# Three pairs' q, k and v in one transfer each, ahead of a unit's stores, with the v casts moved into the Mish stretch

## The chip, the cores and the metric

The kernel runs on one core of a Trainium2 chip. The metric is device time of the whole kernel in microseconds (us); lower is better. The engines are named as the profile names them: PE is TensorE (PEld its weight loads), DVE is VectorE, ACT is ScalarE, POOL is GpSimd, SP is SyncE, which issues nearly all DMA transfers.

## The reference

Attention over 8 batches, 12 heads, 448 positions and a head size of 64, with an extra `exp(-m)` in the softmax's denominator, followed by a two-layer network with Mish between the layers (768 to 2048 to 768, on 3584 tokens). Inputs and output are float32.

```python
scale = 1.0 / np.sqrt(q.shape[-1])
scores = scale * np.matmul(q, k.transpose(0, 1, 3, 2))
m = np.max(scores, axis=-1, keepdims=True)
e = np.exp(scores - m)
attn = e / (np.sum(e, axis=-1, keepdims=True) + np.exp(-m) + 1e-09)
attn_out = np.matmul(attn, v)
x = attn_out.transpose(0, 2, 1, 3).reshape(B * S, H * D)
h = x @ w_in
sp = np.where(h > 20.0, h, np.log1p(np.exp(np.minimum(h, 20.0))))
out = (h * np.tanh(sp)) @ w_out
```

## The kernel before, in words

Work goes by pairs of heads: 48 pairs (`N_PAIRS`), six to a batch. Three pairs (`UNIT_PAIRS`) make a unit, so a batch has two units and the kernel 16 (`N_UNITS`), numbered here from `u` = 0. After a head of two units done pair by pair, each pass of the loop over `u` does three things at once: the scores, maxima, exponentials and sums of unit `u`; the product of its predecessor's attention with v (line 423); and pieces of the network for earlier batches, which fill TensorE between the scores (`fill`, line 543 for the second layer). The second half of a unit is the Mish stretch: eight steps `f`, each with six products of line 442 and a Mish on ScalarE (line 481), between which the next unit is made ready. The order on every engine is the order of the program text (`tc.manual_schedule()`); from the seventh unit on (`u` = 6, `JOINED_FROM`) the first half of a unit follows a list written by hand, `JOINED`.

A pair's way into a unit:

- `load_pair` (line 149) issues three transfers on SP, for q, k and v, 224 KB each (112 partitions, 2 heads, runs of 1 KB), into tiles of a pool with four buffers. In the units with `u` over 4 (`first_mm2`), all the three pairs of the next unit are loaded, one each at the three entries `("load", 0)`, `("load", 1)` and `("load", 2)` of `JOINED` (in the sixth unit, at steps 0, 3 and 6). The stores of finished output rows (line 507) come from the same queue, at the entries `copy`.
- `cast_pair` (line 190) turns q, k and v into bf16 on POOL, in that order (lines 201 or 203, 207 and 188). The first pair is cast at the second load entry, the second pair at the third, the third pair at step `f` = 1 of the Mish stretch.
- q and k are then transposed, either by eight matmuls on TensorE (line 224; four for q, then four for k), at `f` = 3 for the second pair and at `f` = 5 for the third, or by one DMA on SP (`turn_by_dma`, line 237), which a unit's first pair takes from the eighth unit on (turned in the unit before it). In the last unit the second pair goes by DMA too. `rest_of` (lines 245 and 246) copies two small blocks of each pair on POOL.

A unit's own weights leave by `normalise` (line 369): seven operations on DVE (line 386) for the first pair at `f` = 0, seven for the second at `f` = 3, and seven on POOL (line 384) for the third at `f` = 4. Each is followed by a DMA transposition into `eT` on SP (line 390). So SP's queue holds, for each unit in turn: loads, stores, the turned pair, three `eT` transpositions, and then the next unit's loads.

Of the kernel before, what the change touches and what calls it, by code (L numbers as in the profile page):

```python
# [9 lines left out]
FP32 = mybir.dt.float32  # L10
# [5 lines left out]
UNIT_PAIRS = 3  # L16
# [3 lines left out]
def kernel(  # L20
# [11 lines left out]
    B, H, S, D = q.shape  # L32
# [3 lines left out]
    NT = 4  # L36
    SP_ = S // NT
# [10 lines left out]
    N_PAIRS = B * HP  # L48
# [4 lines left out]
    def pool(name, bufs, space=None):  # L53
        if space is None:
            return ctx.enter_context(tc.tile_pool(name=name, bufs=bufs))
        return ctx.enter_context(tc.tile_pool(name=name, bufs=bufs, space=space))

    PS = bass.MemoryType.PSUM
    singles = pool("singles", 1)
    ld_pool = pool("ld", 4)  # L60
    bf_pool = pool("bf", 9)
    st_pool = pool("st", 5)
    eT_pool = pool("eT", 3)
# [36 lines left out]
    w_in_sb = singles.tile([128, DM_T, d_ff], BF16)  # L100
    w_out_sb = singles.tile([128, FF_T, d_model], BF16)

    N_CAST = 2 * UNIT_PAIRS
    qk_bf = singles.tile([SP_, N_CAST, 2, NT, 2, D], BF16)
    qk_all = singles.tile([128, UNIT_PAIRS, 2, S], BF16)
# [26 lines left out]
    loaded, casted, qkT, att, xT, gT, o_sbs, stats = {}, {}, {}, {}, {}, {}, {}, {}  # L132
# [13 lines left out]
        return mo_free.popleft()  # L146


    def load_pair(p, which="qkv"):
        if p >= N_PAIRS:  # L150
            return
        b, h0 = p // HP, (p % HP) * 2
        tiles = loaded.setdefault(p, [])
        for nm, src in (("q", q), ("k", k), ("v", v)):
            if nm not in which:
                continue
            t = ld_pool.tile([SP_, 2, NT * D], FP32, tag=f"{nm}_f", name=f"{nm}_f")
            nc.sync.dma_start(
                out=t, in_=src[b, h0 : h0 + 2].rearrange("h (p t) d -> p h (t d)", t=NT)
            )  # L160
            tiles.append(t)


    def w_pieces():
# [21 lines left out]

    def cast_v(p):
        nc.gpsimd.tensor_copy(out=casted[p][2], in_=loaded.pop(p)[2])  # L188

    def cast_pair(p, with_v=True):  # L190
        if p >= N_PAIRS:
            return
        q_f, k_f = loaded[p][:2]
        q_bf, k_bf = (qk_bf[:, p % N_CAST, i] for i in range(2))
        v_bf = bf_pool.tile([SP_, 2, NT * D], BF16, tag="v_bf", name="v_bf")
        by_t = "p h (t d) -> p t h d"
        cast_q, cast_k = nc.gpsimd.tensor_copy, nc.gpsimd.tensor_copy
        if p == 0:
            cast_q, cast_k = nc.vector.tensor_copy, nc.scalar.copy
        if p not in SCALED_IN_CAST:  # L200
            cast_q(out=q_bf, in_=q_f.rearrange(by_t, t=NT))  # L201
        else:
            nc.gpsimd.tensor_scalar(  # L203
                out=q_bf, in0=q_f.rearrange(by_t, t=NT),
                scalar1=SCALE, scalar2=1.0, op0=ALU.mult, op1=ALU.mult,
            )
        cast_k(out=k_bf, in_=k_f.rearrange(by_t, t=NT))  # L207
        casted[p] = (q_bf, k_bf, v_bf)
        if with_v:
            cast_v(p)  # L210
# [23 lines left out]
    def turn_by_dma(p):  # L234
# [331 lines left out]
    first_mm2 = 2 * UNITS_PER_B  # L566
# [85 lines left out]
    LEAD = UNIT_PAIRS + 1  # L652
    LOAD_AT = (0, 3, 6)
# [33 lines left out]
    for p in range(UNIT_PAIRS):  # L687
        cast_v(p)
# [32 lines left out]
    for u in range(UNITS_PER_B, N_UNITS + 2 * UNITS_PER_B):  # L721
# [10 lines left out]
        nxt = p0 + UNIT_PAIRS  # L732
# [5 lines left out]
        for what, arg in JOINED if joined else ():  # L738
            at, idx = p0 + arg, p0 * STEPS + arg
            heads = {"A": (0,), "B": (1,)}.get(what[-1], (0, 1))  # L740
            if what == "s":
                held[arg] = score_products(idx)
            elif what[0] == "m":
                score_maxima(*held[arg], heads)
            elif what[0] == "e":
                exps(idx, heads)
            elif what == "fill":
                for _ in range(arg):
                    filler.popleft()[0]()
            elif what == "copy":  # L750
                for evac in copies[arg]:
                    evac()
            elif what == "av":
                held["av", arg] = av_pair(at - UNIT_PAIRS, bank=joined_banks[AV_BANK[arg]])
            elif what == "avc":
                held["av", arg]()
            elif what == "load":
                load_pair(at + LEAD - 1)
                if arg:
                    cast_pair(at + LEAD - 2)  # L760
            elif nxt + arg in TURN_BY_DMA:
                turn_by_dma(nxt + arg)
        if joined:
# [2 lines left out]
        for n in () if joined else range(steps):  # L766
            pi, s = divmod(n, STEPS)
            p, idx = p0 + pi, p0 * STEPS + n
            late_tp = u == UNITS_PER_B and n == STEPS
            if late_tp:  # L770
                transpose_pair(p0 + 2)
            exps(idx)
            if grouped:
                order = GROUPED_LATE_AV if u == LATE_AV else GROUPED
                flush_late()
                for what, arg in order[n]:
                    if what == "fill":
                        for _ in range(min(arg, len(filler))):
                            fn, w = filler.popleft()
                            fn()  # L780
                            done += w
                    elif what in ("av0", "av1"):
                        late.append(av_pair(p0 - UNIT_PAIRS + arg, bank=sc_banks[int(what[2])][0]))
                    else:
                        flush_late()
                        for i in arg:
                            scores(p0 * STEPS + i)
                if n in LOAD_AT:
                    at = p0 + LOAD_AT.index(n)
                    if u > first_mm2:  # L790
                        load_pair(at + LEAD - 1)
                        if n:
                            cast_pair(at + LEAD - 2)
                    elif n < LOAD_AT[-1]:
                        load_pair(at + LEAD)
                        cast_pair(at + LEAD - 1)
                if u - UNITS_PER_B < len(W_AT):
                    load_w(W_AT[u - UNITS_PER_B].get(n, 0))
                if n in TURN_AFTER and nxt + TURN_AFTER.index(n) in TURN_BY_DMA:
                    turn_by_dma(nxt + TURN_AFTER.index(n))  # L800
                continue
            if late_tp:
                evac_qk(p0 + 2, act=True)
            if u == UNITS_PER_B + 1:
                for i, part in enumerate(TURN_AT[1].get(n, [])):
                    turn_on_pe(*part)
                    if n == 0:
                        mm1_ahead(0, FIRST_AHEAD[i])
            flush_late()
            acc += weight[n]  # L810
            want = int(total * acc / sum(weight) + 1e-6)
            while done < want:
                fn, w = filler.popleft()
                fn()
                done += w
            scores_ahead(end)
            if n in LOAD_AT:
                load_pair(p0 + LOAD_AT.index(n) + LEAD)
                cast_pair(p0 + LOAD_AT.index(n) + LEAD - 1)
            if u - UNITS_PER_B < len(AV_AT):  # L820
                early = AV_AT[u - UNITS_PER_B]
                if n in early:
                    late.append(av_pair(early[n], act=early[n] in AV_BY_ACT))
                if u == UNITS_PER_B:
                    for part in TURN_AT[0].get(n, []):
# [9 lines left out]
        b, w = (u - UNITS_PER_B) // UNITS_PER_B, u % UNITS_PER_B  # L835
# [5 lines left out]
        for f in range(FF_U):  # L841
# [4 lines left out]
            if moe:  # L846
# [4 lines left out]
                elif to_group:  # L851
                    at = (FIRST_MISH_BANK if first else MISH_BANK)[f]
# [73 lines left out]
```

## Time and profile before

| What | Value |
|---|---|
| median of 3 runs | 462.56 us (461.56 to 463.87) |
| the profiled execution, its own time | 464.11 us |
| its span on the core | 462.3 us |
| PE busy | 427.4 us (92%) |
| DVE, ACT, POOL busy | 340.9, 342.1, 187.3 us |
| granted TensorE clock over the run | 0.987 |
| read from and written to HBM | 45.61 MB, 11.01 MB |

The span is what the trace covers; the profiled execution's own time is 1.8 us longer. The profile's views used below are the page's first part (busy time by engine), the windows (busy time of each engine in a stretch), the timeline of one engine (start and length in us, then what it is, and in brackets how long the engine was idle before and what released it), and the instructions of one line. Times in windows and timelines count from the span's start.

### The profile page before, as it was taken

Reading aid. Unit: us, or ns where it says so; the run is one execution under the profiler, and the core shown is the slowest. Engines: PE = TensorE matmul, PEld = TensorE weight load, DVE = VectorE, ACT = ScalarE, POOL = GpSimd, SP = SyncE. Lnnn points to the kernel's source line nnn. Section 1 sums busy time; section 2 is a strip of 40 time slices with the busy share of each in tenths; the row PEclk is TensorE's granted clock in tenths of the full one; section 3 lists DMA queues with packets and bytes.
Section 4 is the critical chain, followed back from the end, with each engine's and each line's share of the span. In section 5 each row is a group of like instructions: output and inputs, shape, how many; then the busy total and the mean of one; then the engine's idle time right before and its main releaser. Section 6 shows DMA issues by size and latency. Waiting matters only on the chain.

```text
span 462.3 us, 8732 instructions
## 1 busy us (share of the span) xinstructions
PE 427.4 (92%) x2968; PEld 234.3 (51%) x2968; DVE 340.9 (74%) x756; ACT 342.1 (74%) x908; POOL 187.3 (41%) x352
## 2 busy tenths in 40 slices
PE   4596798869999999899999999999999999999996
PEld 2243445434545655455555555455555455555565
DVE  4899978948887888868788888788888888421121
ACT  5998978967797979778888788798988888311300
POOL 4666655652616253353627171625454360000000
PEclk9997999999999999999999999999999999999999
DMA  8999999999999999999999999999999995950213
GB/s 229 207 200 221 255 151 215 221 199 216 195 246 238 207 210 204 264 194 278 199 244 231 219 234 209 271 206 238 227 270 205 255 203 137 171 137 0 69 35 102
DMA packets 211661, 92.66 MB, mean 200 GB/s; under 512 B 168352, under 2 KB 208160, under 8 KB 211616
## 3 DMA queue, kind: packets, MB, share of 16 engines
q1 hardware_dynamic: 204032, 85.76, 87.9%
q0 software_dynamic: 7488, 6.29, 9.4%
q8 instruction: 23, 0.38, 0.4%
q14 instruction: 22, 0.18, 0.1%
q10 hardware_dynamic: 96, 0.05, 0.0%
HBM read 45.61 MB, written 11.01 MB: 122 GB/s over the span
## 4 chain that ended last, share of the span: by engine, by line
PE 65%; DMA 16%; DVE 5%; ACT 5%; issue 3%; SPq 3%; POOL 2%; POOLq 0%; DVEq 0%; ACTq 0%
PE mo L543 25%; PE mo L442 15%; DMA q_f<-in_q_dram 7%; PE b L442 6%; PE b L543 5%; PE b L304 4%; ACT en L347 4%; DMA k_f<-in_k_dram 4%; DMA eT<-en 4%; DVE negm L335 3%; PE b L423 2%; PE mo L423 2%; PE b L224 2%; DMA qk_all<-qk_bf 1%; SPq L390 1%
## 5 line engine op out<-in xcount | busy, mean ns | idle before, releaser
L347 ACT ACTIVATE en<-b,negm 128x448 bf16<-128x448 f32 x216 | 133.9, 636 | 25.7 <-DVE negm L335 25.7
L335 DVE TENSOR_REDUCE negm<-b 128x1 f32<-128x448 f32 x216 | 120.9, 616 | 20.0 <-PE b L307 20.0
L543 PE MATMUL mo<-w_out_sb,gT 128*128 128x384 bf16 (+3 forms) x736 | 108.7, 300 | 1.4 <-DVE o_sb L522 0.7
L543 PEld LDWEIGHTS <-gT 128*128 128x128 bf16 x896 | 82.6, 98 | 51.8 <-issue 10.8
L442 PEld LDWEIGHTS <-w_in_sb 128*128 128x128 bf16 x768 | 72.3, 98 | 66.5 <-issue 5.5
L442 PE MATMUL mo<-xT,w_in_sb 128*128 128x448 bf16 x480 | 101.1, 353 | 0.8 <-DVE xT L432 0.3
L481 ACT ACTIVATE gT<-mo 128x448 bf16<-128x448 f32 x73 | 40.3, 552 | 52.1 <-PE mo L442 52.0
L384 POOL TENSOR_SCALAR en<-en,rden 128x448 bf16<-128x448 bf16 x109 | 67.3, 634 | 19.5 <-DVE rden L378 11.8
L386 DVE TENSOR_SCALAR en<-en,rden 128x448 bf16<-128x448 bf16 x227 | 71.8, 386 | 0.7
L442 PE MATMUL b<-xT,w_in_sb 128*128 128x448 bf16 x282 | 58.7, 352 | 0.0
L347 ACT ACTIVATE en<-sc,negm 128x448 bf16<-128x448 f32 x84 | 52.5, 642 | 3.9 <-DVE negm L335 2.6
L522 DVE COPY o_sb<-mo 128x384 f32<-128x384 f32 (+3 forms) x54 | 25.8, 494 | 40.1 <-PE mo L543 39.4
L335 DVE TENSOR_REDUCE negm<-sc 128x2 f32<-128x896 f32 (+1 forms) x48 | 45.4, 969 | 6.4 <-PE sc L307 4.0
L203 POOL TENSOR_SCALAR qk_bf<-q_f 112x512 bf16<-112x512 f32 x18 | 11.1, 615 | 88.1 <-DMA q_f<-in_q_dram 88.1
L347 ACT ACTIVATION_READ_ACCUMULATOR en<-b,negm 128x1 f32 x216 | 45.0, 208 | 0.0
L201 POOL CAST qk_bf<-q_f 112x512 bf16<-112x512 f32 x29 | 19.7, 679 | 44.6 <-DMA q_f<-in_q_dram 44.2
L188 POOL CAST v_bf<-v_f 112x512 bf16<-112x512 f32 x48 | 30.1, 626 | 15.0 <-DMA v_f<-in_v_dram 14.7
L207 POOL CAST qk_bf<-k_f 112x512 bf16<-112x512 f32 x47 | 29.3, 623 | 7.6 <-DMA k_f<-in_k_dram 6.4
L423 PEld LDWEIGHTS <-v_bf 112*64 112x64 bf16 x384 | 20.1, 110 | 23.4 <-issue 9.0
L224 PEld LDWEIGHTS <-qk_bf 112*128 112x128 bf16 x304 | 19.6, 104 | 21.7 <-POOL qk_bf L207 4.6
L304 PE MATMUL b<-qk_all 64*128 64x448 bf16 x108 | 29.3, 358 | 0.3 <-DMA qk_all<-qk_bf 0.3
L307 PE MATMUL b<-qk_all 64*128 64x448 bf16 x108 | 29.3, 358 | 0.0
(71 smaller groups left out, 524.7 us busy)
## 6 DMA issues: line engine op xcount, KB each, us to landing
q_f<-in_q_dram SPq DMA_DIRECT2D x48, 224.0 KB, 5.4
k_f<-in_k_dram SPq DMA_DIRECT2D x48, 224.0 KB, 5.6
v_f<-in_v_dram SPq DMA_DIRECT2D x48, 224.0 KB, 5.6
w_in_sb<-in_moe_w_in_dram POOLq DMA_DIRECT2D x12, 256.0 KB, 6.3
w_out_sb<-in_moe_w_out_dram POOLq DMA_DIRECT2D x8, 384.0 KB, 6.9
out_dram<-o_sb SPq DMA_DIRECT2D x7, 336.0 KB, 5.2
out_dram<-o_sb SPq DMA_DIRECT2D x8, 288.0 KB, 4.9
out_dram<-o_sb SPq DMA_DIRECT2D x8, 240.0 KB, 5.2
```

The costliest lines, as they stand in the source:

```text
L188: nc.gpsimd.tensor_copy(out=casted[p][2], in_=loaded.pop(p)[2])
L207: cast_k(out=k_bf, in_=k_f.rearrange(by_t, t=NT))
L304: nc.tensor.matmul(sc[0][:, 0:S], lhsT=qT[0:64, qa : qa + 128], rhs=kA, start=True, stop=True)
L307: nc.tensor.matmul(sc[1][:, 0:S], lhsT=qT[64:128, qb : qb + 128], rhs=kB, start=True, stop=True)
L335: nc.vector.tensor_reduce(out=negm, in_=scored, axis=AX.X, op=ALU.max, negate=True)
L347: nc.scalar.activation(out=st["en"][:, :, c, 0:SP_], in_=sc[bk][:, 0:S].rearrange("q (j c) -> q j c", j=NT), func=AF.Exp, bias=st["negm"][ ...
L384: nc.gpsimd.tensor_scalar(scalar2=1.0, op0=ALU.mult, op1=ALU.mult, **args)
L386: nc.vector.tensor_scalar(scalar2=None, op0=ALU.mult, **args)
L423: nc.tensor.matmul(av[h * 64 : (h + 1) * 64, 0:S], lhsT=v_bf[:, h, j * D : (j + 1) * D], rhs=e_h, start=(j == 0), stop=(j == NT - 1),)
L442: nc.tensor.matmul(h_ps[:, 0:S], lhsT=w_in_sb[:, dm, ff * 128 : (ff + 1) * 128], rhs=xT[b][:, dm, :], start=(dm == 0), stop=(dm == DM_T - 1),)
L481: nc.scalar.activation(out=gT[b][:, ff, :], in_=h_ps[:, 0:S], func=AF.Mish)
L543: nc.tensor.matmul(st["o"][:, st["at"] : st["at"] + nq * NQ], lhsT=src[:, ff, c0 : c0 + 128], rhs=w_out_sb[:, ff, q0 * NQ : (q0 + nq) * NQ ...
```

## The change

The pool of load tiles is replaced by one tile each for q, k and v with four slots. In the units from the sixth on (`u` over 4) the first load entry issues one transfer for q, one for k and one for v, each for all three pairs of the next unit (672 KB); the two other load entries issue none. The second entry casts q and k of the first pair, the third entry q and k of the second and third pairs. The three v casts come at `f` = 1 of the Mish stretch, where the third pair's casts stood. Units before the sixth load and cast as they did, into the slots. On PE, DVE and ACT the instructions and their order are the same in both kernels; SP issues 60 fewer loads, and POOL's casts come in the order q, k, q, k, q, k, v, v, v.

```diff
-    ld_pool = pool("ld", 4)
...
+    N_LD = UNIT_PAIRS + 1
+    ld = {
+        nm: singles.tile([SP_, N_LD, 2, NT * D], FP32, tag=f"{nm}_f", name=f"{nm}_f")
+        for nm in "qkv"
+    }
...
-    def load_pair(p, which="qkv"):
+    def load_pair(p, which="qkv", pairs=1):
...
-        tiles = loaded.setdefault(p, [])
+        at = 0 if pairs > 1 else p % N_LD
...
             nc.sync.dma_start(
-                out=t, in_=src[b, h0 : h0 + 2].rearrange("h (p t) d -> p h (t d)", t=NT)
-            )
-            tiles.append(t)
+                out=ld[nm][:, at : at + pairs].rearrange("p s h x -> p (s h) x"),
+                in_=src[b, h0 : h0 + 2 * pairs].rearrange("h (p t) d -> p h (t d)", t=NT),
+            )
+            for i in range(pairs):
+                loaded.setdefault(p + i, []).append(ld[nm][:, at + i])
...
+    def load_and_cast(nxt, step):
+
+        if nxt >= N_PAIRS:
+            return
+        if step == 0:
+            load_pair(nxt, pairs=UNIT_PAIRS)
+        elif step == 1:
+            cast_pair(nxt, with_v=False)
+        else:
+            for p in range(nxt + 1, nxt + UNIT_PAIRS):
+                cast_pair(p, with_v=False)
...
             elif what == "load":
-                load_pair(at + LEAD - 1)
-                if arg:
-                    cast_pair(at + LEAD - 2)
+                load_and_cast(nxt, arg)
...
                     if u > first_mm2:
-                        load_pair(at + LEAD - 1)
-                        if n:
-                            cast_pair(at + LEAD - 2)
+                        load_and_cast(nxt, LOAD_AT.index(n))
...
-                if f == 1 and u >= first_mm2:
+                if f == 1 and u == first_mm2:
                     cast_pair(nxt + UNIT_PAIRS - 1)
+                elif f == 1 and u > first_mm2 and nxt < N_PAIRS:
+                    for p in range(nxt, nxt + UNIT_PAIRS):
+                        cast_v(p)
```

More of the change, by code (lines that the diff above doesn't have):

```diff
@@ L156, in load_pair @@
                 continue
-            t = ld_pool.tile([SP_, 2, NT * D], FP32, tag=f"{nm}_f", name=f"{nm}_f")
             nc.sync.dma_start(
-                out=t, in_=src[b, h0 : h0 + 2].rearrange("h (p t) d -> p h (t d)", t=NT)
-            )
-            tiles.append(t)
+                out=ld[nm][:, at : at + pairs].rearrange("p s h x -> p (s h) x"),
+                in_=src[b, h0 : h0 + 2 * pairs].rearrange("h (p t) d -> p h (t d)", t=NT),
+            )
+            for i in range(pairs):
+                loaded.setdefault(p + i, []).append(ld[nm][:, at + i])
     def w_pieces():
```

## The prediction

> **What bounds the kernel now.** I read the page first, then the stretches of nine like units, then one unit in order of time, engine by engine.
>
> ```profile
> span 462.3 us, 8732 instructions
> PE 427.4 (92%) x2968; PEld 234.3 (51%) x2968; DVE 340.9 (74%) x756; ACT 342.1 (74%) x908; POOL 187.3 (41%) x352
> ```
>
> TensorE is busy 92% of the span, so a change of loads can only give back the gaps between TensorE's work, or add to them. The stretches run from one unit's first `mo` product of line 543 to the next unit's, for the seventh to the fifteenth unit; the columns are length, then the busy time of each engine.
>
> ```profile
> 149.74:174.15 24.41, 24.41 (x174) 13.55 (x175) 21.11 (x49) 20.91 (x57) 9.93 (x21) 1.00 1.01 205
> 174.15:200.58 26.43, 24.74 (x174) 13.47 (x175) 20.53 (x48) 21.01 (x57) 12.22 (x24) 1.00 1.08 239
> 275.10:300.26 25.16, 24.57 (x175) 13.55 (x175) 21.01 (x48) 21.01 (x57) 11.65 (x24) 1.00 1.16 236
> sum 224.48, PE 220.80 PEld 121.20 DVE 188.30 ACT 188.37 POOL 101.34; mean PE 24.53 PEld 13.47 DVE 20.92 ACT 20.93 POOL 11.26
> ```
>
> A unit without a wait takes 24.41 us (first row). Nine take 224.48, so 224.48 - 9 x 24.41 = 4.8 us, 0.53 a unit, is all that the nine lose. Where it is lost is seen in the unit of the third row, in the DMA queue of SP:
>
> ```profile
> 270.38 13.56 SPq L390 DMA_TRANSPOSE eT<-en  x3
> 284.00 0.57 SPq L158 DMA_DIRECT2D q_f<-in_q_dram  x1
> ...
> 286.61 0.46 SPq L158 DMA_DIRECT2D v_f<-in_v_dram  x1
> 287.17 2.27 SPq L507 DMA_DIRECT2D out_dram<-o_sb  x4
> 289.74 0.66 SPq L158 DMA_DIRECT2D q_f<-in_q_dram  x1
> 290.67 0.34 SPq L158 DMA_DIRECT2D k_f<-in_k_dram  x1
> 291.60 0.31 SPq L158 DMA_DIRECT2D v_f<-in_v_dram  x1
> 292.27 1.26 SPq L237 DMA_TRANSPOSE qk_all<-qk_bf  x1
> 295.20 13.73 SPq L390 DMA_TRANSPOSE eT<-en  x3
> 308.98 0.57 SPq L158 DMA_DIRECT2D q_f<-in_q_dram  x1
> ```
>
> The first load leaves the moment the third `eT` transposition has been issued. I call this T0 (284.00) and count from it. Two pairs' loads leave by +3.1, then four stores, and the third pair's only at +5.7 to +7.9. The three `eT` transpositions hold SP for 13.73 us; the next T0 follows at once. So T0 is set by the first `eT`, and that by the first normalisation. POOL and TensorE in the same unit:
>
> ```profile
> 287.86 0.62 POOL L203 TENSOR_SCALAR qk_bf<-q_f 112x512 bf16<-112x512 f32 x1 [9.21 <-DMA q_f<-in_q_dram]
> 288.79 0.61 POOL L207 CAST qk_bf<-k_f 112x512 bf16<-112x512 f32 x1 [0.31 <-DMA k_f<-in_k_dram]
> 289.84 0.61 POOL L188 CAST v_bf<-v_f 112x512 bf16<-112x512 f32 x1 [0.44 <-DMA v_f<-in_v_dram]
> 290.71 0.61 POOL L201 CAST qk_bf<-q_f 112x512 bf16<-112x512 f32 x1 [0.26 <-DMA q_f<-in_q_dram]
> 291.64 0.61 POOL L207 CAST qk_bf<-k_f 112x512 bf16<-112x512 f32 x1 [0.31 <-DMA k_f<-in_k_dram]
> 292.32 0.61 POOL L188 CAST v_bf<-v_f 112x512 bf16<-112x512 f32 x1
> 295.19 0.61 POOL L201 CAST qk_bf<-q_f 112x512 bf16<-112x512 f32 x1 [2.26 <-DMA q_f<-in_q_dram]
> 296.14 0.75 POOL L207 CAST qk_bf<-k_f 112x512 bf16<-112x512 f32 x1 [0.34 <-DMA k_f<-in_k_dram]
> 296.84 0.65 POOL L188 CAST v_bf<-v_f 112x512 bf16<-112x512 f32 x1
> ```
>
> ```profile
> 293.33 0.56 PE L224 MATMUL b<-ident,qk_bf 112*128 112x112 bf16 x8
> ...
> 296.00 0.36 PE L224 MATMUL b<-ident,qk_bf 112*128 112x112 bf16 x4
> 296.95 0.37 PE L224 MATMUL b<-ident,qk_bf 112*128 112x112 bf16 x4 [0.59 <-POOL qk_bf L207]
> ```
>
> The second pair's k was cast by 292.25 (+8.3), its transposes came at +9.3, without a wait. The third pair's k was cast at 296.89, and TensorE stood 0.59 us for it. This is the wait that the change is aimed at.
>
> **What goes.** The third pair's q and k no longer queue behind stores, and the v casts no longer lie between the q and k casts. At best this wait goes in all nine units: 4.8 us, 1.0%. Fewer instructions on SP (three loads for nine) give nothing by themselves: T0 hangs on the `eT` chain. If the issue of a transfer three times as large took three times as long, 1.4 us for 0.46, three would be out at +4.2, still before the stores are needed. The stores leave earlier or at the same place in the queue, and nothing waits for them.
>
> **What moves later: the second pair.** All casts are in POOL's order q0, k0, q1, k1, q2, k2, and k0 now waits for the whole k transfer: the sixth piece of 224 KB on the queue. The nearest rows for when six pieces have landed are in the seventh unit, whose loads began at 157.88:
>
> ```profile
> 157.88 0.57 SPq L158 DMA_DIRECT2D q_f<-in_q_dram  x1
> ...
> 161.45 0.62 POOL L203 TENSOR_SCALAR qk_bf<-q_f 112x512 bf16<-112x512 f32 x1 [9.18 <-DMA q_f<-in_q_dram]
> ...
> 164.08 0.61 POOL L188 CAST v_bf<-v_f 112x512 bf16<-112x512 f32 x1 [1.36 <-DMA v_f<-in_v_dram]
> ...
> 166.36 0.61 POOL L188 CAST v_bf<-v_f 112x512 bf16<-112x512 f32 x1 [0.20 <-DMA v_f<-in_v_dram]
> ```
>
> POOL was waiting for v of the first pair (third piece) until +6.2 and for v of the second (sixth piece) until +8.5; in the unit above the fifth piece was there at +7.6 and the sixth by +8.3. I take +8.2 for k, between 7.6 and 8.5, and 10.6 for v, at the same pace (2.4 us for three pieces). Then k0, q1, k1 at 0.62: k1 is ready at 8.2 + 3 x 0.62 + 0.1 for two hand-overs (296.89 to 296.95 is one) = 10.1, where TensorE wants it at 9.53 (293.33 plus 0.2 for the first four). That is a wait of 0.57 at the second pair, with the 0.59 at the third gone: k2 is ready at 11.4, before the third pair comes. One wait takes the place of another, worth +0.04 a unit against today's mean of 0.53.
>
> The bigger transfer could be cheaper. The Trainium skill's "DMA: Bandwidth & Descriptors" (section "Anatomy of one DMA — SWDGE (gpsimd) path") fits a DMA's time as 2.0 us plus bytes by 436 GB/s: by it q would land at 3.6 and k at 5.2. The rows do not agree: by that fit three pieces behind each other would also be there at 3.6, and they took 5.8 and 6.2.
>
> **What gets dense: POOL beside the first normalisation.** Today POOL rests from 292.93 to 295.19, and the first normalisation of DVE lies just there; the second lies beside casts:
>
> ```profile
> 293.32 1.81 DVE L386 TENSOR_SCALAR en<-en,rden 128x448 bf16<-128x448 bf16 x7
> ...
> 295.35 2.78 DVE L386 TENSOR_SCALAR en<-en,rden 128x448 bf16<-128x448 bf16 x7
> ```
>
> ```profile
> L386 DVE TENSOR_SCALAR en<-en,rden x3: 323/677/678, 245.8 to 246.6; 128x448 bf16<-128x448 bf16 x3
> ```
>
> Seven take 1.81 us alone, 2.78 beside about three casts. In the unit at 245.8 those beside a cast took 0.677, those clear of one 0.323: 0.35 us for each. After the change POOL casts without a break from 8.25: five to 11.4, and the three v casts after them to 13.3. The first normalisation starts at 9.3 (293.32), in the middle of it. If all seven meet a cast it takes 7 x 0.35 = 2.45 us longer; none, 0. Call this x. The first `eT`, today 0.07 us behind it (295.13 to 295.20), is late by x, and so is the next T0 with all its loads. The second normalisation meets casts today too, so I put nothing there; the turn of the first pair (line 237) waits for k0, 8.9 for 8.27, and ends at 10.2, before the first `eT`.
>
> The Trainium skill's "SBUF — State Buffer" (section "Who interferes with whom") says that such a DVE operation and a POOL one lock each other out for a whole instruction. By turns of 0.61 and 0.26 (1.81 for seven) each of the seven would then take 0.87, and x would be 4.3. The rows agree that DVE is held up, but a held one takes 0.677, waiting and all, and the casts grow only to 0.65 to 0.75, so I keep 2.45 as the top.
>
> **The sum.** Let TensorE come to the second pair's k at A after T0, and wait s = 10.1 - A. The next T0 lies at A - 0.21 (start of the normalisation) + 1.81 + x + 0.07 + 13.78 (295.20 to 308.98) = A + 15.45 + x; TensorE comes to its next second pair at A + s + 24.41. So the next A = 8.96 + s - x. In balance A = 9.53 - x/2 and s = 0.57 + x/2. Half of any delay of T0 is paid in each unit, as TensorE's wait also moves the next normalisation. Against today's 0.53 a unit the nine units lose 9 x (0.04 + x/2).
>
> x = 0 gives +0.4 us, x = 2.45 gives +11.4. The balance is not reached smoothly: a late T0 lets TensorE come early after it, the next normalisation then begins before 8.25 and partly misses the casts, and the unit after meets them in full. So I take two thirds, x = 1.6: 9 x 0.84 = +7.6 us. The profiled execution took 464.11 us (its span and 1.8 around it), 1.55 above the median of the three; I put the change on the median: 462.56 + 7.6 = **470.2 us**. A change of under 0.5% (2.3 us) can't be told from none here.
>
> **The rivals.**
> - *One wait for another, no collision* (x near 0, because DVE's seven slip between casts or POOL waits for v before going on): 462.56 + 0.4 = 463.0. For it: the wait at the second pair alone is about as long as the one that goes. Against it: five casts in a row lie over 9.3 to 11.1 wherever k lands between 7.6 and 8.5. Chance 0.18.
> - *Faster: the pieces land at the pace of their issue.* First piece at 3.5 (161.45), five more at 0.5 each: k at 6.0, k1 ready at 7.96. The casts of q and k end at 9.2 and v's, which wait for no store any more, follow to 11.1; x is about four casts, 1.4. A = 8.96 + s - 1.4 and s = 7.96 - A give s = 0.2: 9 x (0.2 - 0.53) = -3.0, 459.6. For it: stores no longer share the engines with the first six pieces. Against it: pieces three to six took 0.8 each with their issue long past. Chance 0.09. It decides as soon as k lands before about 6.5.
> - *Slower by more* (x over 2.45, or the turn of the first pair late into the scores): up to 474 and past it. Chance 0.05.
>
> That the change does something other than it says is not left open: the order of the instructions shows three loads of 672 KB a unit ahead of the stores, the same work on TensorE, DVE and ACT, and only POOL's casts in a new order.
>
> **How the numbers follow.** The forecast has 0.68. The range goes from 462.2, just under the first rival, to 474.2, the top of x (462.56 + 11.4 = 474.0); it leaves out the faster case and the far slower end, about 0.15. Slower by over 0.5% is the forecast and the far end, 0.73; the same is the first rival, 0.18; faster 0.09. Within the forecast alone the range is 465 to 474.2.
>
> **What would show it.** In the profile after: TensorE's wait for the third pair gone, a wait of line 224 at the second pair instead; POOL's first cast at +6, then five without a break from +8.2; the first normalisation (line 386, seven) at 3 us and more for 1.81; T0 to T0 grown to 25.5 and over. If the seven still take 1.8 and units stay at 24.9, the first rival holds; if k is cast by +6.5, the second.

## The result, and the profile after

The changed kernel takes 475.0 us (median of 4 executions, 472.88 to 475.25), against 462.43 us for the kernel before beside it: ratio 1.026, 95% interval 1.022 to 1.030. It is slower, as forecast, but by 12.6 us where 7.6 were forecast. In a later session, where it was run again beside an experiment, four more executions gave a median of 469.53 us and a ratio of 1.019 (1.010 to 1.028); the kernel before took the same in both (462.43 and 462.82 us), and what the traces say of the difference stands below.

The profiled execution took 475.25 us. The first lines of its page, and the line with the chain of work that ended last (line numbers are 3 to 17 higher than before: the loads are line 161, the casts 193, 218, 220 and 224, the transposes 241, DVE's normalisation 403, the eT transposition 407, the stores 524, the mo product 560):

```profile
span 473.1 us, 8658 instructions
PE 437.4 (92%) x2968; PEld 238.7 (50%) x2968; DVE 349.7 (74%) x756; ACT 342.8 (72%) x908; POOL 184.2 (39%) x352
...
PE mo L560 20%; PE mo L459 16%; DMA k_f<-in_k_dram 12%; SPq L407 7%; PE b L459 7%; DVE negm L352 4%; PE b L321 3%; ACT en L364 2%; PE mo L440 2%; PE b L241 2%; PE b L560 2%; POOL qk_bf L224 2%; DMA eT<-en 1%; PE mo L418 1%; PE b L440 1%
```

The k transfer now carries 12% of the chain; before, q's carried 7% and k's 4%, so about the same share of the chain lies on loads as before, moved to k. And TensorE is busy 10.0 us longer than the 427.4 us of before, with the same 2968 instructions: part of the loss is not waiting but slower work. The windows of the nine like units (length, then busy time of PE, PEld, DVE, ACT and POOL, then PEclk, the granted clock: the share of full speed at which TensorE was allowed to run, then DMA share and GB/s) show where:

```profile
148.91:173.70 24.79, 24.56 (x176) 13.62 (x174) 22.22 (x49) 21.29 (x57) 9.59 (x21) 1.00 1.05 201
173.70:202.71 29.01, 26.41 (x175) 14.07 (x174) 20.91 (x48) 20.91 (x57) 14.06 (x28) 0.94 1.11 229
...
253.18:281.66 28.48, 26.42 (x175) 13.94 (x173) 22.61 (x49) 21.22 (x57) 13.45 (x27) 0.94 1.08 208
...
357.27:385.12 27.85, 26.04 (x167) 13.53 (x166) 22.50 (x48) 20.58 (x56) 10.88 (x22) 0.94 1.09 208
sum 236.21, PE 226.66 PEld 122.73 DVE 196.42 ACT 189.28 POOL 98.58; mean PE 25.18 PEld 13.64 DVE 21.82 ACT 21.03 POOL 10.95
```

The nine units take 236.21 us for 224.48: +11.7. The stretch ahead of them is 0.8 shorter than before (148.91 for 149.74) and what follows is as long (473.1 - 385.12 = 88.0 for 88.1), which gives the spans' difference of 10.8. So all of it is in the nine units. Half of their +11.7 is idle time (236.21 - 226.66 = 9.55 for 3.7 before), half is busy time (226.66 for 220.80), and the latter lies in the three units whose clock is 0.94.

One unit in order of time shows the steps that were forecast. SP's queue, with T0 at 340.96:

```profile
340.96 0.59 SPq L161 DMA_DIRECT2D q_f<-in_q_dram  x1
341.61 0.56 SPq L161 DMA_DIRECT2D k_f<-in_k_dram  x1
342.21 0.52 SPq L161 DMA_DIRECT2D v_f<-in_v_dram  x1
342.83 3.17 SPq L524 DMA_DIRECT2D out_dram<-o_sb  x4
350.09 1.23 SPq L254 DMA_TRANSPOSE qk_all<-qk_bf  x1
353.89 13.66 SPq L407 DMA_TRANSPOSE eT<-en  x3
367.60 0.57 SPq L161 DMA_DIRECT2D q_f<-in_q_dram  x1
```

POOL and DVE in the same unit (start, length, and in brackets the idle time before and what ended it):

```profile
347.21 0.62 POOL L220 TENSOR_SCALAR qk_bf<-q_f 112x512 bf16<-112x512 f32 x1 [11.46 <-DMA q_f<-in_q_dram]
349.46 0.61 POOL L224 CAST qk_bf<-k_f 112x512 bf16<-112x512 f32 x1 [1.63 <-DMA k_f<-in_k_dram]
350.01 0.69 POOL L218 CAST qk_bf<-q_f 112x512 bf16<-112x512 f32 x1
...
351.85 0.65 POOL L224 CAST qk_bf<-k_f 112x512 bf16<-112x512 f32 x1
352.45 1.84 POOL L193 CAST v_bf<-v_f 112x512 bf16<-112x512 f32 x3
```

```profile
349.89 3.93 DVE L403 TENSOR_SCALAR en<-en,rden 128x448 bf16<-128x448 bf16 x7
```

q is cast at +6.25, k of the first pair at +8.5, then POOL casts without a break to +13.3. The seven normalising operations start at +8.9 and take 3.93 us beside these casts, for 1.81 alone; the first `eT` leaves 0.07 us after them, and the next T0 comes 26.64 us after this one. That is the collision. What follows a long wait is seen on TensorE in an earlier unit:

```profile
273.47 0.37 PE L241 MATMUL b<-ident,qk_bf 112*128 112x112 bf16 x4 [1.83 <-POOL qk_bf L218]
274.06 0.37 PE L241 MATMUL b<-ident,qk_bf 112*128 112x112 bf16 x4 [0.23 <-POOL qk_bf L224]
274.27 2.01 PE L459 MATMUL mo<-xT,w_in_sb 128*128 128x448 bf16 x6
276.07 2.32 PE L459 MATMUL b<-xT,w_in_sb 128*128 128x448 bf16 x6
278.23 0.56 PE L241 MATMUL b<-ident,qk_bf 112*128 112x112 bf16 x8
```

The wait is at the second pair; the third pair's eight transposes (278.23) wait for nothing. But the second six products of line 459 take 2.32 us. Elsewhere in the same trace six take 1.30:

```profile
376.70 1.30 PE L459 MATMUL b<-xT,w_in_sb 128*128 128x448 bf16 x6
```

The windows of 3.41 us around this place:

```profile
267.84:271.26 3.42, 3.42 (x20) 1.76 (x18) 2.19 (x6) 3.40 (x10) 0.62 (x1) 1.00 1.13 231
271.26:274.67 3.41, 1.35 (x13) 0.63 (x12) 3.41 (x10) 2.48 (x6) 2.52 (x4) 1.00 0.85 222
274.67:278.08 3.41, 3.41 (x11) 1.43 (x10) 3.20 (x8) 0.93 (x2) 3.25 (x9) 0.51 1.10 200
278.08:281.50 3.42, 3.42 (x28) 1.69 (x26) 0.39 (x1) 1.93 (x4) 3.32 (x7) 0.99 1.16 178
```

After a stretch in which TensorE was idle for 2.06 us of 3.41, the next 3.41 us ran at a granted clock of 0.51. Such a stretch follows the three longest waits, 2.41, 1.83 and 1.59 us, in the three units with PEclk 0.94. Each costs half of its 3.4 us, 1.7 us: an estimate of 5.1 in all.

### The profile page after: what moved, and what is told of

Read it like the earlier page. It is cut to its first block, busy times and chain, and to the rows that moved or that the text cites. A ratio compares the mean times of both kernels' runs of the same rounds, so it can differ in the third digit from the quotient of the medians.

```text
span 473.1 us, 8658 instructions
## 1 busy us (share of the span) xinstructions
PE 437.4 (92%) x2968; PEld 238.7 (50%) x2968; DVE 349.7 (74%) x756; ACT 342.8 (72%) x908; POOL 184.2 (39%) x352
## 4 chain that ended last, share of the span: by engine, by line
PE 56%; DMA 13%; SPq 8%; DVE 6%; ACT 3%; POOL 3%; issue 2%; ACTq 0%
PE mo L560 20%; PE mo L459 16%; DMA k_f<-in_k_dram 12%; SPq L407 7%; PE b L459 7%; DVE negm L352 4%; PE b L321 3%; ACT en L364 2%; PE mo L440 2%; PE b L241 2%; PE b L560 2%; POOL qk_bf L224 2%; DMA eT<-en 1%; PE mo L418 1%; PE b L440 1%
## 5 line engine op out<-in xcount | busy, mean ns | idle before, releaser
L560 PE MATMUL mo<-w_out_sb,gT 128*128 128x384 bf16 (+3 forms) x736 | 107.5, 298 | 1.5 <-DVE o_sb L539 0.9
L459 PEld LDWEIGHTS <-w_in_sb 128*128 128x128 bf16 x768 | 73.5, 99 | 69.3 <-issue 10.1
L459 PE MATMUL mo<-xT,w_in_sb 128*128 128x448 bf16 x480 | 103.6, 359 | 0.7 <-DVE xT L449 0.3
L403 DVE TENSOR_SCALAR en<-en,rden 128x448 bf16<-128x448 bf16 x227 | 79.4, 418 | 0.7
L459 PE MATMUL b<-xT,w_in_sb 128*128 128x448 bf16 x282 | 60.9, 362 | 0.1
L440 PE MATMUL mo<-eT,v_bf 112*64 112x448 bf16 x232 | 28.4, 382 | 1.0 <-DVE eT L422 0.6
L321 PE MATMUL b<-qk_all 64*128 64x448 bf16 x108 | 29.1, 354 | 0.2 <-DVE qk_all L280 0.2
L560 PE MATMUL b<-w_out_sb,gT 128*128 128x384 bf16 x160 | 29.3, 326 | 0.0
```

What stands on the lines that cost most here:

```text
L321: nc.tensor.matmul(sc[0][:, 0:S], lhsT=qT[0:64, qa : qa + 128], rhs=kA, start=True, stop=True)
L403: nc.vector.tensor_scalar(scalar2=None, op0=ALU.mult, **args)
L440: nc.tensor.matmul(av[h * 64 : (h + 1) * 64, 0:S], lhsT=v_bf[:, h, j * D : (j + 1) * D], rhs=e_h, start=(j == 0), stop=(j == NT - 1),)
L459: nc.tensor.matmul(h_ps[:, 0:S], lhsT=w_in_sb[:, dm, ff * 128 : (ff + 1) * 128], rhs=xT[b][:, dm, :], start=(dm == 0), stop=(dm == DM_T - 1),)
L560: nc.tensor.matmul(st["o"][:, st["at"] : st["at"] + nq * NQ], lhsT=src[:, ff, c0 : c0 + 128], rhs=w_out_sb[:, ff, q0 * NQ : (q0 + nq) * NQ ...
```

## The experiments

The theory (A): k waits for a transfer that lands at +8.4 to +8.6, so that POOL's casts become one dense run over the first normalisation; this delays `eT` and the next T0, and TensorE waits at the second pair; a long wait then costs another 1.7 us, because the clock is halved after it. The rivals: (B) the size of the transfer itself, or the queue, costs the time, and the collision is harmless; (C) the half clock only takes time that would have been waited anyway; (D) another transfer becomes late as soon as the casts are early. Line numbers in the rows of experiments differ by a few from one kernel to the next.

**The two halves of the change apart.** First the loads alone: three merged transfers ahead of the stores, and the casts in the old order q, k, v, pair by pair.

```diff
         if step == 0:
             load_pair(nxt, pairs=UNIT_PAIRS)
-        elif step == 1:
-            cast_pair(nxt, with_v=False)
         else:
-            for p in range(nxt + 1, nxt + UNIT_PAIRS):
-                cast_pair(p, with_v=False)
+            cast_pair(nxt + step - 1)
...
-                if f == 1 and u == first_mm2:
+                if f == 1 and u >= first_mm2:
                     cast_pair(nxt + UNIT_PAIRS - 1)
-                elif f == 1 and u > first_mm2 and nxt < N_PAIRS:
-                    for p in range(nxt, nxt + UNIT_PAIRS):
-                        cast_v(p)
```

> The other part alone: one transfer each for q, k and v of three pairs ahead of the stores, but POOL casts q, k, v pair by pair as before. The first v cast now waits for the whole v transfer (about 10.6), and the second pair's q and k stand behind it: k1 ready at about 12.6. Theory A: waits at the second pair of 2 to 3 us in most units, several of them long enough for the half clock: 482 to 492 us. A theory in which the merged transfers themselves cost the time: about as the changed kernel, 473 to 477.

485.53 us (2 executions), ratio 1.048 (1.038 to 1.058): theory A's time. POOL and TensorE:

```profile
192.23 0.61 POOL L221 CAST qk_bf<-k_f 112x512 bf16<-112x512 f32 x1 [3.35 <-DMA k_f<-in_k_dram]
194.50 0.61 POOL L193 CAST v_bf<-v_f 112x512 bf16<-112x512 f32 x1 [1.66 <-DMA v_f<-in_v_dram]
195.05 0.61 POOL L215 CAST qk_bf<-q_f 112x512 bf16<-112x512 f32 x1
```

```profile
195.72 1.11 PE L238 MATMUL b<-ident,qk_bf 112*128 112x112 bf16 x8 [4.61 <-POOL qk_bf L215]
```

POOL stands at the first pair's v, behind which the second pair's q lies ready; TensorE waits 4.61 us, and its eight transposes take 1.11 us (0.56 above): the half clock again. Now the other half, the v casts moved and the loads as they were:

```diff
         if step == 0:
-            load_pair(nxt, pairs=UNIT_PAIRS)
+            load_pair(nxt)
         elif step == 1:
+            load_pair(nxt + 1)
             cast_pair(nxt, with_v=False)
         else:
+            load_pair(nxt + 2)
             for p in range(nxt + 1, nxt + UNIT_PAIRS):
                 cast_pair(p, with_v=False)
```

> One part of the change alone: the loads stay as before (one pair at a time, the third behind the stores), only the casts are in the new order, v of all three pairs in the Mish stretch. The third pair's q lands at about 11 as before, so its casts end where they did. Theory A: less of the casting meets the first normalisation (v of the second pair is gone from there), more the second: 461 to 464 us, the same as before. A rival (v casts at that place delay POOL's own normalisation and with it the third transposition): 466 us or more.

461.87 us, ratio 0.999 (0.995 to 1.003): no difference that can be told. The nine units of its profile take 222.38 us, and its normalisations are 1.81 to 2.5 us long:

```profile
sum 222.38, PE 220.39 PEld 121.64 DVE 191.88 ACT 188.12 POOL 101.93; mean PE 24.49 PEld 13.52 DVE 21.32 ACT 20.90 POOL 11.33
```

So the loads carry the whole cost; moving the v casts is neutral by itself and takes half of the loads' cost away again, or more (ratio 1.048 alone, 1.026 and 1.019 together with it).

**Is it the size of a transfer?** Nine transfers of 224 KB, in the order of the merged ones and at their place; casts as in the changed kernel.

```diff
         if step == 0:
-            load_pair(nxt, pairs=UNIT_PAIRS)
+            for nm in "qkv":
+                for i in range(UNIT_PAIRS):
+                    load_pair(nxt + i, nm)
```

> The changed kernel with each of its three transfers cut into three of one pair (q q q k k k v v v), same place ahead of the stores, same casts. k of the first pair is then the fourth piece. Theory A: k0 at about 7 for 8.6, the run of casts starts earlier but still lies over the first normalisation: k1 ready at about 8.7, x about 2, 0.9 us of waits a unit: 465 to 467 us. Theory B (only the moment of k): k1 ready 1.5 us earlier than in the changed kernel, before TensorE comes: 460 to 463 us. If the size of a transfer costs nothing by itself (it lands as its last piece would) both hold; if big transfers are slower by themselves, the last k piece lands earlier than 8.6.

465.55 us, ratio 1.008 (1.004 to 1.012): theory A's time. In a unit with T0 at 207.52:

```profile
214.87 0.61 POOL L226 CAST qk_bf<-k_f 112x512 bf16<-112x512 f32 x1 [3.46 <-DMA k_f<-in_k_dram]
215.42 0.66 POOL L220 CAST qk_bf<-q_f 112x512 bf16<-112x512 f32 x1
```

The first pair's k is cast at +7.35 here. Over the nine units its transfer lands at 6.0 to 8.3 and the third pair's k at 7.4 to 10.1, where the merged transfer lands at 7.7 to 10.1. So a merged transfer is not slow; it is there when its last third would be, and the first third waits for it. Without that waiting the ratio is 1.008, for 1.019 to 1.026 with it. The rest stays: the normalisation still meets the casts (2.2 to 4.0 us), and the nine units take 227.4. Rival B is out for the transfer's size, but not for the late k.

**Is it the collision?** The merged transfers as they are, but the third pair's q and k casts and the v casts held until DVE has done the first normalisation, by a tiny copy on POOL that reads its last output.

```diff
+    gate = singles.tile([128, 2], BF16)
...
-        elif step == 1:
-            cast_pair(nxt, with_v=False)
         else:
-            for p in range(nxt + 1, nxt + UNIT_PAIRS):
-                cast_pair(p, with_v=False)
+            cast_pair(nxt + step - 1, with_v=False)
...
                 elif f == 1 and u > first_mm2 and nxt < N_PAIRS:
+                    nc.gpsimd.tensor_copy(
+                        out=gate, in_=att[todo[0]]["en"][:, 0, NTILE - 1, 0:2]
+                    )
+                    cast_pair(nxt + UNIT_PAIRS - 1, with_v=False)
                     for p in range(nxt, nxt + UNIT_PAIRS):
                         cast_v(p)
```

> The changed kernel, with one more wait: the third pair's q and k and the three v are cast after the seventh operation of the first normalisation (a copy of two columns on POOL reads its result). k of the second pair is ready no earlier than in the changed kernel (10.1 after the first load), k of the third later. Theory A (casts without a break hold up the first normalisation, which sets the next unit's loads; and a long wait of TensorE is followed by 3.4 us at half clock): only one or two casts meet the first normalisation, x falls from up to 2.45 to about 0.5, the waits at the second pair stay under 1.2 us, no stretch of half clock in these units: 466 to 469 us. Theory B (k landing late is all there is to it, what DVE loses beside casts is on no path): the second pair comes no earlier and the third later, so 475 us or more.

468.16 us, ratio 1.014 (1.007 to 1.020): theory A's time. Against the changed kernel's 1.026 that is a gain, against its 1.019 in the later session it can't be told from none; its nine units take 230.39 us, and the changed kernel's two profiles have 236.21 and 229.87. So this run alone does not show what the collision costs. POOL rests while DVE normalises:

```profile
243.66 0.70 POOL L222 CAST qk_bf<-k_f 112x512 bf16<-112x512 f32 x1
245.78 0.19 POOL L888 COPY gate<-en 128x2 bf16<-128x2 bf16 x1 [1.42 <-DVE en L401]
245.91 0.61 POOL L216 CAST qk_bf<-q_f 112x512 bf16<-112x512 f32 x1
```

The first normalisation is 1.81 to 2.87 us long (mean 2.20, as before the change, 2.19). The late k stays, and with it waits up to 2.08 us, where under 1.2 were expected; one of 1.84 us brought a stretch of half clock, where none was expected.

**Neither the late k nor the collision.** Two runs. In the first, nine small transfers, q and k pair by pair and then the three v, ahead of the stores; in the second the v casts are held by the copy as well.

```diff
         if step == 0:
-            load_pair(nxt, pairs=UNIT_PAIRS)
+            for i in range(UNIT_PAIRS):
+                load_pair(nxt + i, "qk")
+            for i in range(UNIT_PAIRS):
+                load_pair(nxt + i, "v")
```

> The changed kernel with nine transfers of one pair ahead of the stores in the order q k, q k, q k, then v v v; same casts. Theory A: q and k are cast as they land and are all ready by about 9.0; the v casts (pieces seven to nine, 9.2 to 10.4) meet about three of the first normalisation's operations, x about 1; no wait of TensorE for casts at all: 458 to 460 us, faster than both. A theory that the stores behind all loads, or the load tiles in one piece, cost time of their own: 463 us or more.

464.63 us, ratio 1.005 (1.001 to 1.009), where 458 to 460 were expected. No wait for a cast was left, but two things were. The v casts took the place of the q and k casts over the normalisation (2.5 to 3.6 us). And the first pair, turned by DMA behind the stores, came late to the scores:

```profile
190.61 3.64 DVE L406 TENSOR_SCALAR en<-en,rden 128x448 bf16<-128x448 bf16 x7
...
222.38 0.36 PE L324 MATMUL b<-qk_all 64*128 64x448 bf16 x1 [1.58 <-DMA qk_all<-qk_bf]
...
sum 224.46, PE 220.23 PEld 121.57 DVE 192.40 ACT 188.55 POOL 100.45; mean PE 24.47 PEld 13.51 DVE 21.38 ACT 20.95 POOL 11.16
```

With the v casts held:

```diff
+    gate = singles.tile([128, 2], BF16)
...
                 elif f == 1 and u > first_mm2 and nxt < N_PAIRS:
+                    nc.gpsimd.tensor_copy(
+                        out=gate, in_=att[todo[0]]["en"][:, 0, NTILE - 1, 0:2]
+                    )
                     for p in range(nxt, nxt + UNIT_PAIRS):
                         cast_v(p)
```

> The kernel with nine transfers, q k by pair first and then the v, and in addition the three v casts wait for the first normalisation's seventh operation. Theory A: the only casts left beside the first normalisation are those of the second and third pair's q and k that have not ended when it starts (end at 9 to 9.7), so its seven take 1.8 to 2.9 us for 2.5 to 3.6, the next loads leave in time, and the waits for the turned pair and for v's partner go with it: 24.5 us a unit, 458 to 460 us against 462.4 of before. Theory D (the waits for the turned pair come from its place in the DMA queue behind the v loads and the stores, not from the lateness of the unit's loads): they stay at 1.2 to 1.6 us in two units, and the time at 462 to 464.

459.48 us (12 executions), ratio 0.994 (0.990 to 0.997): theory A's time, and by its interval a little faster than the kernel before. The nine units take 222.26 us; the normalisation is back at 1.81 to 2.5.

```profile
sum 222.26, PE 219.63 PEld 121.57 DVE 190.44 ACT 188.52 POOL 100.35; mean PE 24.40 PEld 13.51 DVE 21.16 ACT 20.95 POOL 11.15
```

```profile
192.43 1.81 DVE L407 TENSOR_SCALAR en<-en,rden 128x448 bf16<-128x448 bf16 x7
...
223.75 0.36 PE L325 MATMUL b<-qk_all 64*128 64x448 bf16 x1 [1.41 <-DMA qk_all<-qk_bf]
```

It differs by the held v casts alone from the run before it, whose ratio was 1.005: the collision with three v casts cost 1.1%, each measured against the kernel before in its own session. In the two profiles the nine units show 2.2 us of it (224.46 for 222.26), 0.5%; where the rest lies is not shown. The wait for the turned pair stays (theory D). So that pair was turned earlier, right behind the q and k loads, ahead of the v loads and the stores:

```diff
         if step == 0:
             for i in range(UNIT_PAIRS):
                 load_pair(nxt + i, "qk")
-            for i in range(UNIT_PAIRS):
-                load_pair(nxt + i, "v")
         elif step == 1:
             cast_pair(nxt, with_v=False)
+            if nxt in TURN_BY_DMA:
+                turn_by_dma(nxt)
+            for i in range(UNIT_PAIRS):
+                load_pair(nxt + i, "v")
...
-            elif nxt + arg in TURN_BY_DMA:
+            elif arg and nxt + arg in TURN_BY_DMA:
                 turn_by_dma(nxt + arg)
```

> The kernel of the run with the held v casts, and the first pair is turned by DMA right behind the six q and k transfers, ahead of the v loads and the stores. Theory A: the turned pair lands by about 11 for 14, nothing waits for it; as the run with held v casts, or 1 us faster: 457 to 460 us. Theory D: this is the run in which the waits for the turned pair go, 458 to 460, where the run with held v casts does not. A rival against both: the turn makes the v loads and the stores later, and the first transposition into eT queues behind them: 463 us or more.

461.62 us, ratio 0.996 (0.992 to 0.999): slower than both theories expected, faster than the rival, and not to be told from the run before it. The wait for the turned pair is gone, as theory D had it, but the `eT` of one unit came late, long enough to bring half clock; the run before it waited 0.67 us at the same place, and whether the earlier turn made the difference is not shown:

```profile
262.88 0.95 PE L446 MATMUL mo<-eT,v_bf 112*64 112x448 bf16 x8 [1.81 <-DMA eT<-en]
```

```profile
248.31:276.35 28.04, 26.23 (x175) 13.97 (x173) 21.05 (x49) 21.27 (x57) 13.70 (x28) 0.94 1.03 224
```

**The half clock.** The changed kernel, with five products that nothing reads ahead of the waiting transposes, in every one of the units that follow the written list:

```diff
                 if nxt + f // 2 not in TURN_BY_DMA:
+                    if joined and f == (5 if nxt + 1 in TURN_BY_DMA else 3):
+                        for _ in range(5):
+                            nc.tensor.matmul(
+                                sc_banks[1][1][:, 0:S], lhsT=w_in_sb[:, 0, 0:128],
+                                rhs=w_in_sb[:, 0, 0:S], start=True, stop=True,
+                            )
                     transpose_pair(
```

> The changed kernel with five products of 448 columns with no reader on TensorE (about 0.95 us) right ahead of the transposes that wait for the second pair (in the fifteenth unit, the third). The three waits of 2.4, 1.8 and 1.6 us become 1.5 or less. Theory A with its half clock after long waits: no stretch at half clock in these units, up to 3 x 1.7 us back, less 0.95 us in each of the two or three units that have no wait: 471 to 474 us. If the half clock does not hang on the length of the wait, or its loss is only taken from the next wait: 475 us or more, with stretches at half clock as before.

473.41 us, ratio 1.027 (1.021 to 1.032). The nine units had no half clock and took 232.85 us, 3.4 less than the changed kernel's first profile; but the products take 0.95 us in each of nine units, and no gain is left in the ratio. So the same in the three units with the long waits alone (`u in (7, 10, 14)` for `joined`), and the changed kernel itself beside it:

> The changed kernel, with five products of 448 columns that nothing reads ahead of the waiting transposes in three units only: the eighth, eleventh and fifteenth, where the changed kernel's profile has waits of 2.41, 1.83 and 1.59 us, each followed by 3.4 us at granted clock 0.5. The five take 0.95 us and lie inside the waits, so they put nothing on the path if those units wait as before. Theory A (a wait of about 1.8 us and more in one 3.4 us window costs the wait and then 1.7 us more at half clock): no half clock in these three units, their waits cut to 0.6 to 1.5 us, the nine units at 231 us for 236.2 in the changed kernel's profile, and the kernel 3 to 5 us under the changed kernel run beside it: 470 to 472 us if that takes 475. Theory B (the half clock only takes time that TensorE would have waited away later anyway): no half clock in the three, but longer waits in the units after them, and the same time as the changed kernel within 1.5 us.

> The changed kernel once more, unaltered, as the measure for the run beside it: 473 to 477 us, ratio 1.022 to 1.030, nine units of about 236 us, and three stretches of 3.4 us at granted clock 0.5 in them, each behind a wait of 1.6 us or more. If its profile has none, or has them in other units, the place of the dips is a matter of the single execution.

With the products 473.87 us, ratio 1.024 (1.015 to 1.034); without them 469.53, ratio 1.019 (1.010 to 1.028), where 473 to 477 were expected. The run with products had no half clock and 231.52 us in its nine units, as theory A expected, but it was no faster than the changed kernel beside it: neither theory's expectation was met, because the changed kernel's second profile had no half clock in the nine units to take away. That profile answers the question in another way. It took 466.29 us, and its windows of the same three units as above, with their sum:

```profile
170.63:197.19 26.56, 24.74 (x176) 13.47 (x174) 22.14 (x48) 21.23 (x57) 11.97 (x24) 1.00 1.10 237
...
247.64:274.68 27.04, 24.93 (x176) 13.54 (x174) 22.70 (x49) 21.22 (x57) 11.32 (x23) 1.00 1.02 212
...
351.79:376.11 24.32, 24.18 (x168) 13.24 (x166) 21.78 (x48) 20.80 (x56) 10.04 (x21) 1.00 1.03 213
sum 229.87, PE 221.99 PEld 121.45 DVE 198.55 ACT 189.72 POOL 98.38; mean PE 24.66 PEld 13.49 DVE 22.06 ACT 21.08 POOL 10.93
```

The same kernel, the same collision (its first normalisations take 2.52 to 4.24 us), 229.87 us instead of 236.21; in the three units PE is busy 1.67, 1.49 and 1.86 us less, 5.0 of the 6.3. This speaks against rival C: without half clock the time was not waited elsewhere; idle time was lower, too (7.9 us for 9.55). It is one profile against one. That the products prevent the half clock was not shown.

The nine units are not the whole difference between the two profiles of the changed kernel: 2.7 us lie ahead of them (148.91 us for 146.24), in a stretch that takes 145.7 to 150.2 us over the twelve profiles of all kernels here. How much of that is clock is not shown.

All eight executions of the changed kernel fit the same picture: 475.25, 475.06, 474.93, 472.88, 472.32, 470.88, 468.17 and 466.29 us had mean granted clocks of 0.967, 0.967, 0.971, 0.985, 0.982, 0.978, 0.988 and 0.992. The mean does not say where the clock was lost; in the first profile 20.5 of 31.2 us at half clock lie ahead of the nine units, most of them in its first 60 us. A straight line through the eight gives 470.0 us at 0.985. One through 60 executions of the kernel before, which cover 0.973 to 0.996, gives 463.2 there, and 462.7 without the 12 longest of their sessions: +6.9 to +7.3 at the same clock, an estimate close to the forecast's +7.6. Why the clock was lower in the first session than in the second stays open.

## Why the prediction was right in its direction and wrong in its size

By its own steps:

- **The wait moves from the third pair to the second.** Right: line 241 waits at the second pair in five of the nine units, and at the third only in the last of the nine, which turns its second pair by DMA. These waits make 8.9 us with the short ones for k behind them. Before, the waits of the transposes made 3.4 us; the 4.8 us that the forecast took for this wait hold other waits and units with a little more work, too.
- **k lands as the sixth piece, at +8.2.** Nearly: 8.6 in the mean, 7.7 to 10.1; 8.4 in the second profile. Issuing a merged transfer took 0.5 to 0.6 us, not three times an old one's. The fit in the Trainium skill's "DMA: Bandwidth & Descriptors" (section "Anatomy of one DMA — SWDGE (gpsimd) path"), by which k would land at 5.2 by estimate, is given there for DMAs that GpSimd issues; it does not agree with these rows of SP's queue.
- **POOL casts without a break from 8.25 to 13.3 over the first normalisation.** Right, to 0.3 us in the unit shown. That such a collision costs time is shown by the pair of runs with and without the v casts held (ratio 0.994 for 1.005); for the changed kernel itself it is not shown apart from the late k.
- **x, the delay of the first `eT`.** The nine first normalisations last 2.85 us in the mean (1.81 to 3.93), so x = 1.04 over the 1.81 that the balance starts from; 3.49 and 1.68 in the second profile; 1.6 was taken. Before the change they were 2.19, not 1.81: the forecast took the clean one for the common one. T0 to T0 is 26.2 us in the mean, for 25.2 before, and early and late units alternate (25.51, 27.89, 24.96 one after the other), as argued.
- **The balance, s = 0.57 + x/2.** With the measured values it gives 0.57 + (1.04 + 0.4)/2 = 1.29 a unit (0.4 for k at 8.6 and not 8.2), 0.76 over before's 0.53, 6.8 us for nine; the first profile shows 11.7 - 5.1 = 6.6 without its half clock. For the second profile, which had the longer normalisations, it gives 8.8, and 5.4 were measured. It is good to about 3 us, and the close fit of the first profile is in part luck.
- **"Against today's 0.53 a unit the nine units lose 9 × (0.04 + x/2)", put on the median of before.** This is the step that failed. It priced a wait at its length and put a lower clock at nothing. In these traces idle time of about 1.8 us or more within one 3.41 us step mostly costs 1.7 us more (last section), and the change makes waits of that length: the longest in the nine units was 1.50 us before, 2.41 after. The three stretches in the first profile cost 5.1 us; without them it would show +6.6, a little under the forecast's +7.6. The second profile of the same kernel had no such stretch in the nine units and shows +5.4 in them, at 466.29 us. So the waiting was forecast about right, and the clock's share was between nothing and 5 us. Of the other three executions behind the 475.0 us only the mean clock is known (0.967, 0.971 and 0.985, for 0.967 in the profiled one).

Of the rivals, the one without collision falls by the 3.93 us of the row above, the one with k landing by +6.5 by the casts at +8.5. The far slower end (x over 2.45, or the turned pair late) has the measured time, but not for its reason: x was 1.04. A quicker version exists (0.994), but by loads in small pieces, q and k first, and the v casts held, which the forecast did not weigh.

## What to carry to other kernels

In this kernel the first part of a merged transfer could be used only when the last had landed; an engine that works in order then stood, and did all its work in one dense run, over whatever was there. Order small transfers by who needs them first, and hold back what nobody waits for (here the v casts) until the neighbour that they slow down is through (here DVE's normalisation). Price a wait of TensorE not by its length alone: see in the trace whether the granted clock falls after it, and judge a kernel with such waits by many executions, not by one profile.

## What the runs showed of the hardware

The granted clock changes on a grid. In every trace the stretches at 0.5 begin on steps of 3.413 us counted from each other. I summed TensorE's idle time within each such step, from 125 us on to 20 us before the end, over the twelve profiles of this study. Nine steps that followed full clock had 1.81 us idle or more; after eight of them (1.81, 1.81, 1.96, 2.06, 2.07, 2.93, 3.02, 3.30) the next step ran at half clock, after one (1.98) it did not. After all 19 steps with 1.2 to 1.76 us it did not. So what counts is not the wait's length but how much idle time falls in one step; the exception shows that this is not all. The longest wait of the run with products in three units was cut in two by the grid:

```profile
345.83 0.37 PE L241 MATMUL b<-ident,qk_bf 112*128 112x112 bf16 x4 [2.08 <-POOL qk_bf L218]
```

```profile
340.89:344.30 3.41, 2.86 (x16) 1.27 (x13) 2.19 (x9) 3.38 (x9) 0.62 (x1) 1.00 1.13 232
344.30:347.71 3.41, 1.70 (x14) 1.01 (x15) 2.40 (x7) 1.96 (x5) 3.23 (x6) 1.00 1.09 308
347.71:351.13 3.42, 3.42 (x25) 1.95 (x24) 2.56 (x7) 2.06 (x4) 3.19 (x9) 1.00 1.24 279
```

2.08 us of waiting, 0.55 in one step and 1.71 with the short wait in the next, and no loss of clock; 1.83 us in one step, 2.06 with the short wait, in the first profile, lost it. As the grid lies differently in each execution, the same wait can cost 2 us in one and 3.7 in another (an estimate: 1.7 more). This is one reason why single profiles of the changed kernel disagree. It does not explain the whole spread: the kernel before ran from 457.96 to 467.58 us in one session. Its own profile has a step with 1.69 us idle, close to those that lost the clock, so that it may lose it in other executions; no trace shows that.

The Trainium skill's "TensorE: Matmul & The Clock Gate" (section "What's actually happening") has the free-running window of 3413 ns, and the traces agree with it. It lets the clock fall after at least one idle window of about 3.4 us; here just over half a window of idle time, 1.81 us, was enough, and the measurement decides.
